# Linear attention and a multiplicative FFN on one core: the gate products of the last four chunks by Strassen's seven block products

## The chip, the core and the metric

The kernel runs on one core of a Trainium2 chip. The metric is the device time of one execution in microseconds (us); lower is better. The engines are TensorE (PE, which does all matrix products and writes their sums to PSUM), VectorE (DVE), ScalarE (ACT), GpSimd (POOL) and SyncE (SP, which here issues nearly all DMAs). Each engine works through its own instructions strictly in order, and waits for the others by semaphores. PSUM has eight banks of 128 partitions x 512 f32.

## The reference

```python
phi = lambda x: np.where(x > 0, x, np.exp(x) - 1.0) + 1.0
q_p, k_p = phi(q), phi(k)                       # q, k, v: 8 batches, 8 heads, 576 rows, 64 columns
kv  = einsum('bhsd,bhse->bhde', k_p, v)
num = einsum('bhsd,bhde->bhse', q_p, kv)
den = einsum('bhsd,bhd->bhs', q_p, k_p.sum(axis=2))[..., None] + 1e-06
x   = (num / den) as 4608 tokens x 512
a, b = x @ w1, x @ w2                           # the gates: 512 -> 1024
out = ((a * b) @ w3) @ w_out                    # 4608 x 512, f32
```

## The kernel before

The 4608 tokens are 9 chunks of 512 tokens (`c0` = 0 to 8), each of 4 tiles of 128 tokens (`t` = 0 to 35, `t = 4*c0 + m`). The product of w3 and w_out is formed once (wf), so that an output tile is `(a*b) @ wf`.

All work is written out by hand as a list of steps in the string ORDER (L21 to L61). Each step is a small function; the list is run from left to right, and what it issues stands on every engine's queue in that order. A name such as `F.3.4` is the kind (`s_F`) and its arguments; a last letter is the engine that does the copy (a: ACT, v: DVE, p: POOL, s: SP).

- Loads `LQ`, `LK`, `LV` (L164 to L179): 576 KB each, of q, k, v for one batch and one half of the heads, issued on SP into one of 13 buffers of the kind "ld". A buffer comes free (`give`) when its readers have run.
- `EX` (exp on ACT), `PT` and `PM` (two DVE passes) form phi; `VC` converts v to bf16.
- `KB` is the kv product on PE. `QD` transposes phi(q) of one batch half by a DMA transpose on SP (L386) into one of 4 buffers "qt".
- `NT` (L422) is num and den of three token tiles on PE: 48 small products into both of two double PSUM tiles (kind "at", two banks each), then three short DVE instructions to 1/den. `NM.t.0`, `.1`, `.2` (L437) are the divisions on DVE into "xn", and release the two tiles. `ND` is the same for one token tile.
- `XD.c0.m` transposes two token tiles of a chunk by a DMA transpose on SP (L463) into "xt".
- `F.c0.f` (L497) is one block of 128 of the 1024 gate columns for one chunk: 4 matmuls of 128x512 for a into a bank of the kind "mm" (four banks), 4 for b into another, an ACT copy of a to SBUF (L492), and a DVE product of that copy with b's bank (L494) into the chunk's tile "ab".
- `O.t` (L540) is one output tile: 8 matmuls of 128x512 from "ab" and wf, and a copy of the bank to SBUF by ACT or DVE (L543). `S.t` stores it by two DMAs of 128 KB (L549). `Q.35` is the last tile, in pieces.

PSUM is the four "mm" banks and the two double "at" tiles for the whole run. The first part of the list loads and prepares the weights, and treats batches 0 and 1 and chunk 0. The list of before from the step `PT.k.2.0` on:

```python
LV.3.1 O.3.a PT.k.2.0 LQ.2.0 S.0.s LQ.3.0 PM.k.2.0 PM.q.2.1 VC.2.0.v LV.4.1 F.1.0 F.1.1 PT.k.3.1
PM.q.3.1 VC.3.0.a F.1.2 VC.2.1.a PT.q.2.0 F.1.3 LK.3.0 EX.q.2.0 PM.q.2.0 LQ.5.1 S.1.s S.2.s ND.8
KB.2.a QD.2.0 EX.k.3.1 F.1.4 PT.q.3.0 EX.q.3.0 PT.k.3.0 PM.k.3.1 F.1.5 VC.3.1.v QD.2.1 EX.k.3.0
PM.k.3.0 QD.3.1 F.1.6 F.1.7 O.4.a PM.q.3.0 PT.q.5.1 QD.3.0 NT.9 KB.3.a O.5.a NM.9.0 O.6.a NM.9.1
NM.9.2 NT.12 NM.12.0 NM.12.1 NM.12.2 O.7.a XD.2.0 XD.2.1 LV.4.0 F.2.0 LQ.4.0 EX.q.5.1 F.2.1 NT.15
S.3.s F.2.2 NM.15.0 F.2.3 LK.4.1 F.2.4 PM.q.5.1 F.2.5 VC.4.0.a LQ.4.1 LK.4.0 PT.k.4.0 EX.k.4.0
PM.k.4.0 XD.3.0 PT.k.4.1 F.2.6 F.2.7 XD.3.1 LK.5.1 LK.5.0 F.3.0 PT.q.4.0 PT.q.4.1 F.3.1 EX.q.4.0
F.3.2 PT.k.5.1 LK.7.0 O.8.a PT.k.5.0 EX.k.4.1 NM.15.1 NM.15.2 F.3.3 S.4.s EX.q.4.1 PM.k.4.1 EX.k.5.0
LV.5.1 LV.6.0 S.5.s VC.4.1.v PM.q.4.0 EX.k.5.1 LQ.5.0 LV.5.0 S.6.s PM.k.5.1 F.3.4 PT.q.5.0 PM.q.4.1
S.7.s S.8.s VC.5.0.v O.9.a EX.q.5.0 O.10.a O.11.a LQ.7.1 VC.5.1.v PM.q.5.0 QD.4.0 F.3.5 F.3.6
PM.k.5.0 EX.k.7.0 KB.4.v PT.k.7.0 QD.4.1 S.9.s S.10.s S.11.s F.3.7 KB.5.a NT.18 XD.4.0 O.12.a
PM.k.7.0 NM.18.0 NM.18.1 XD.4.1 QD.5.1 NM.18.2 O.13.a O.14.v O.15.a F.4.0 F.4.1 F.4.2 F.4.3 VC.6.0.a
...
```

Attention (the steps `NT`, `NM`, `QD`) goes on beside the gates of chunks 1 to 7; `NM.33.2`, its last step, stands just before `F.7.0`.

## Time and profile before

| quantity | before |
| --- | --- |
| median of 3 runs | 240.42 us (240.42 to 240.85) |
| span of the profiled execution, first to last instruction | 239.7 us |
| PE busy | 233.2 us (97%) |
| DVE busy | 151.0 us (63%) |
| ACT busy | 115.0 us (48%) |
| POOL busy | 8.1 us (3%) |
| DMA, mean rate | 233 GB/s |

The time of the profiled execution itself is not given apart from its span; the median stands 0.7 us above the span. How to read the profile: the page splits the span into 40 slices of 6 us and gives each engine's busy share in tenths. The groups of instructions give for each line its busy time, the mean duration of one instruction, and the idle time ahead of it with what ended it. The chain of waits follows the end of the run back through whatever released each piece of work. The table by windows gives busy microseconds of each engine in a stretch, then the granted TensorE clock, the share of the 16 DMA engines that was busy (packets in flight side by side can take it above 1) and GB/s.

### The profile page before, as it was taken

What the parts mean: (1) busy time and instruction counts of PE and PEld (TensorE: products, weight loads), DVE (VectorE), ACT (ScalarE), POOL (GpSimd) and SP (SyncE); (2) the same over time, 40 slices, a digit from 0 to 9 for tenths busy, and PEclk for the clock granted to TensorE, in tenths of its full rate; (3) what the DMA queues carried; (4) which work ended last, traced back from release to release, by engine and by line L of the source; (5) the groups of instructions that cost most, each with busy time, mean ns of one, the idle gap of its engine ahead of it and who ended that gap; (6) DMA issues with size and microseconds to landing.
All of it is one profiled execution on the core that took longest, in us unless ns stands there. A gap on an engine that the chain in (4) does not pass through costs nothing.

```text
span 239.7 us, 5540 instructions
## 1 busy us (share of the span) xinstructions
PE 233.2 (97%) x2276; PEld 120.2 (50%) x2276; DVE 151.0 (63%) x278; ACT 115.0 (48%) x173; POOL 8.1 (3%) x15
## 2 busy tenths in 40 slices
PE   8899999999999999999999999999999999999994
...
DVE  0347787889999646877862588885546363433341
...
PEclk9999999999999999999999999999999999999999
DMA  6999999999996999999879959965293763005216
GB/s 241 402 406 397 379 375 390 390 390 389 396 332 137 158 357 247 323 406 296 190 106 192 392 123 262 320 116 131 52 178 69 174 157 88 3 0 125 50 24 154
DMA packets 52553, 55.81 MB, mean 233 GB/s; under 512 B 31280, under 2 KB 32560, under 8 KB 52528
## 3 DMA queue, kind: packets, MB, share of 16 engines
...
q10 hardware_dynamic: 240, 0.26, 0.3%
q14 instruction: 7, 0.06, 0.1%
...
## 4 chain that ended last, share of the span: by engine, by line
PE 96%; DVE 1%; ACT 1%; issue 0%
PE o_ps L536 26%; PE a_ps L483 25%; PE b_ps L483 24%; PE wf_ps L264 6%; PE nd L399 3%; PE w3p L252 3%; PE warm L149 2%; PE kbp L341 2%; PE a_ps L516 2%; PE b_ps L516 2%; PE xp L458 1%; PE qp L369 1%; PE kvp L341 1%; ACT wo_sb L218 0%; ACT w3b L238 0%; DVE w3t L253 0%
## 5 line engine op out<-in xcount | busy, mean ns | idle before, releaser
L483 PEld LDWEIGHTS <-w_sb 128*128 128x128 bf16 x544 | 52.6, 98 | 62.5 <-DVE xt L459 0.3
L494 DVE TENSOR_TENSOR ab<-a_sb,b_ps 128x512 bf16<-128x512 f32 x68 | 46.2, 686 | 39.9 <-PE b_ps L483 38.6
L492 ACT COPY a_sb<-a_ps 128x512 f32<-128x512 f32 x68 | 39.8, 586 | 64.0 <-PE a_ps L483 63.6
L483 PE MATMUL a_ps<-xt,w_sb 128*128 128x512 bf16 x272 | 69.9, 380 | 0.0
L483 PE MATMUL b_ps<-xt,w_sb 128*128 128x512 bf16 x272 | 69.8, 379 | 0.0
L536 PE MATMUL o_ps<-wf_sb,ab 128*128 128x512 bf16 (+2 forms) x304 | 65.2, 368 | 0.0
L536 PEld LDWEIGHTS <-ab 128*128 128x128 bf16 x304 | 28.4, 98 | 31.7 <-issue 0.4
L543 ACT COPY o_sb<-o_ps 128x512 f32<-128x512 f32 x22 | 12.9, 586 | 33.5 <-PE o_ps L536 26.7
L405 DVE TENSOR_TENSOR xn<-nd,r 128x512 bf16<-128x512 f32 (+2 forms) x47 | 23.8, 559 | 0.3
L274 ACT ACTIVATE ek<-k 128x1152 bf16<-128x1152 f32 x16 | 18.7, 1172 | 0.7 <-ACT ek L274 0.7
L274 ACT ACTIVATE eq<-q 128x1152 bf16<-128x1152 f32 x16 | 18.7, 1168 | 0.4 <-DMA q<-in_q_dram 0.4
L543 DVE COPY o_sb<-o_ps 128x512 f32<-128x512 f32 x13 | 9.0, 691 | 15.3 <-PE o_ps L536 12.6
L264 PE MATMUL wf_ps<-wo_sb,w3t 128*128 128x512 bf16 x64 | 15.6, 380 | 0.5 <-ACT wo_sb L218 0.5
L286 DVE TENSOR_SCALAR phq<-q 128x1152 bf16<-128x1152 f32 x16 | 12.0, 755 | 2.7 <-DMA q<-in_q_dram 2.7
L294 DVE TENSOR_TENSOR phk<-phk,ek 128x1152 bf16<-128x1152 bf16 x16 | 11.9, 750 | 1.8 <-ACT ek L274 1.7
L294 DVE TENSOR_TENSOR phq<-phq,eq 128x1152 bf16<-128x1152 bf16 x16 | 12.1, 755 | 1.0 <-ACT eq L274 0.8
L286 DVE TENSOR_SCALAR phk<-k 128x1152 bf16<-128x1152 f32 x16 | 12.0, 753 | 0.0
L264 PEld LDWEIGHTS <-w3t 128*128 128x128 bf16 x64 | 5.9, 98 | 5.8 <-issue 0.7
L328 ACT CAST vt<-v 128x1152 bf16<-128x1152 f32 x7 | 8.1, 1162 | 0.9 <-DMA v<-in_v_dram 0.9
L253 ACT CAST w3t<-w3p 128x512 bf16<-128x512 f32 x7 | 4.0, 587 | 9.3 <-PE w3p L252 7.4
L399 PEld LDWEIGHTS <-qt 64*64 64x64 bf16 x576 | 6.1, 106 | 4.3 <-issue 4.1
L399 PE MATMUL nd<-kv,qt 64*64 64x65 bf16 x576 | 7.6, 194 | 0.4 <-DVE w3t L253 0.4
...
## 6 DMA issues: line engine op xcount, KB each, us to landing
...
v<-in_v_dram SPq DMA_DIRECT2D x16, 576.0 KB, 10.5
...
```

The costliest lines, as they stand in the source:

```text
L264: nc.tensor.matmul(wfs[i], w3ts[i][:, c, :], wo_sb[:, c, :], start=(c == 0), stop=(c == FC - 1))
L274: nc.scalar.activation(out=t, in_=raw[n, b, h], func=AF.Exp)
L286: (nc.gpsimd if e == "p" else nc.vector).tensor_scalar(out=by_set(n, t), in0=by_set("k", raw[n, b, h]), scalar1=0.0, scalar2=1.0, op0=ALU. ...
L294: nc.vector.tensor_tensor(out=t, in0=t, in1=by_set("k", es[n, b, h]), op=ALU.min)
L399: nc.tensor.matmul(dst[g * R:(g + 1) * R], qts[b, a // 2][rows, j, a % 2 * R:(a % 2 + 1) * R], kvs[b][rows, a // 2, a % 2, :], start=True, ...
L405: nc.vector.tensor_tensor(out=xn[:, :, a0:a1], in0=n4[:, :, :, 0:D], in1=r.unsqueeze(3).to_broadcast([P, 2, a1 - a0, D]), op=ALU.mult)
L483: nc.tensor.matmul(ops_[key][:, tiles.start * P:tiles.stop * P], w[:, w_row(kc), f * P:(f + 1) * P], xts[c0][:, tiles, kc, :], start=(kc = ...
L492: nc.scalar.copy(out=a_sbs[c0, f], in_=ops_[key])
L494: nc.vector.tensor_mul(out=abs_[c0][:, f, :], in0=a_sbs[c0, f], in1=ops_[key])
L516: nc.tensor.matmul(p, w[:, w_row(kc), f * P:(f + 1) * P], xts[c0][:, 2 * g:2 * g + 2, kc, :], start=(kc == 0), stop=(kc == KC - 1))
L536: nc.tensor.matmul(o_ps, abs_[c0][:, f, m * P:(m + 1) * P], wf_sb[:, f, cols], start=(f == 0), stop=(f == FC - 1))
L543: copy_of(e)(out=o_sbs[t], in_=o_ps)
```

## The change

The gates of chunks 5 to 8 are formed in two pairs of chunks, (5, 6) and (7, 8). For a pair, each gate is a product of w (512 rows x 1024 columns, as two by two blocks of 256 x 512) with x of the two chunks (two by two blocks of 256 rows x 512 tokens). It is formed by seven block products in place of eight, in Winograd's form of Strassen's scheme, which needs four sums of blocks of w (`WS`, for w1 and w2) and four of blocks of x (`WT`, for each pair).

- A step `WP.c0.f.side.i` is block product i for block column f (0 to 3) and gate `side` (0: a, 1: b): two matmuls of 128x512. Products 1, 6, 7, 4 add up in one bank, 5 and 3 in a second, 2 stands in an "mm" bank. ACT copies the partial sums after products 1, 5, 6 (and, for gate a, after 4) to SBUF in f32. DVE adds such a copy to a bank after 2, 3, 7; for gate b each sum is then multiplied with gate a's in a second DVE instruction, and after 4 with the bank itself. The copies use the buffers of "e", "phk", "phq" and "a_sb".
- `WS` and `WT` are DVE additions and subtractions of 128 x 1024 bf16 in SBUF. The sums of w1 lie in wo_sb, whose first use is over; the other sums and the a*b blocks ("abq") take buffers of the kind "ld", and `O` reads a*b from there.
- `RB` closes the pool of the double tiles "at" and opens four single banks "bk" in their place, for the products. It stands after `NM.33.2`, so that all `NT` and `NM` are ahead of all `WP`.
- The list is new from `PT.k.2.0` on: `F.1` to `F.4`, attention of batches 2 to 7 and its loads and transposes stand ahead of `RB`; the `WP` steps, 20 `O` steps and `Q.35` behind it.

```diff
--- before.py
+++ after.py
+PAIRS = (5, 7)
+WIDE = ()
...
+XP.7.v LV.2.1 EX.k.2.0 PM.k.2.1 LV.3.1 O.3.a PT.k.2.0 PM.q.2.1 LQ.3.0 VC.3.1.v LK.3.0 PM.q.3.1 VC.3.0.a
+VC.2.0.v F.1.5 S.0.s F.1.7 LQ.2.0 EX.q.3.0 PM.k.2.0 LK.5.0 LV.5.1 LK.4.0 LQ.4.0 F.1.1 EX.k.3.0 PT.k.3.1
+PT.q.2.0 S.2.s EX.q.2.0 F.1.2 PT.k.3.0 PM.q.2.0 F.1.4 QD.2.1 VC.2.1.a F.1.6 PT.q.3.0 QD.2.0 ND.8
+PM.k.3.0 LQ.5.1 EX.k.3.1 KB.2.a F.1.0 LQ.4.1 PM.q.3.0 QD.3.1 PM.k.3.1 F.1.3 NT.9 NM.9.0 QD.3.0 NM.9.1
+LQ.5.0 KB.3.a PT.q.4.1 EX.q.5.1 O.7.a NM.9.2 EX.q.4.0 VC.5.1.v XD.2.0 S.1.s O.6.a PT.k.4.0 PT.q.5.1
+NT.12 EX.k.5.0 PT.k.5.0 XD.2.1 O.5.a NM.12.0 LV.4.1 PM.q.5.1 O.4.a PT.q.5.0 NM.12.1 NM.12.2 LK.4.1
+PT.q.4.0 EX.q.4.1 F.2.7 NT.15 LK.5.1 NM.15.0 LK.6.1 LK.6.0 LV.4.0 EX.k.4.1 WS.1.1.v F.2.5 XD.3.1
+VC.4.1.v PM.q.4.0 S.7.s PM.k.5.0 F.2.6 F.2.2 PM.q.4.1 F.2.4 WS.0.1.v LV.5.0 F.2.3 EX.k.4.0 WS.1.3.v
+PT.k.4.1 VC.4.0.a PM.k.4.0 XD.3.0 PT.k.5.1 F.2.1 LV.6.0 S.4.s S.5.s EX.q.5.0 PM.q.5.0 S.3.s LQ.7.0 F.3.4
+PM.k.4.1 F.2.0 NM.15.1 LQ.7.1 F.3.7 NM.15.2 EX.k.5.1 VC.5.0.v KB.4.v PM.k.5.1 WS.1.2.v QD.4.0 QD.4.1
+LV.7.1 EX.k.6.0 O.8.a PT.q.7.1 EX.k.6.1 PT.k.6.0 F.3.2 NT.18 WS.0.3.v LQ.6.1 QD.5.1 NM.18.0 LQ.6.0 S.8.s
+XD.4.0 KB.5.a VC.6.0.a F.3.5 PT.k.6.1 PM.k.6.0 F.3.3 EX.q.7.1 LK.7.0 PT.q.6.1 O.9.a NM.18.1 QD.5.0
+PT.q.7.0 NM.18.2 PM.k.6.1 S.6.s VC.7.1.v EX.q.7.0 PT.k.7.0 LK.7.1 F.3.6 XD.4.1 PT.q.6.0 O.10.a O.11.a
+EX.q.6.1 LV.6.1 NT.21 NM.21.0 F.4.1 NM.21.1 VC.6.1.v LV.7.0 F.3.1 PM.q.7.1 NM.21.2 F.3.0 XD.5.1 KB.6.v
+NT.24 EX.q.6.0 PM.q.6.0 PM.q.7.0 EX.k.7.1 QD.7.1 PM.q.6.1 S.11.s XD.5.0 F.4.2 WS.1.4.v NM.24.0 QD.6.0
+F.4.3 QD.6.1 WS.0.2.v EX.k.7.0 PM.k.7.0 S.10.s F.4.7 S.9.s PT.k.7.1 F.4.0 PM.k.7.1 NM.24.1 XD.6.0
+VC.7.0.a F.4.4 QD.7.0 NM.24.2 F.4.5 F.4.6 NT.27 NM.27.0 KB.7.a NM.27.1 NM.27.2 O.19.a NT.30 XD.6.1
+NM.30.0 NM.30.1 O.13.a NM.30.2 WT.5.1.v WT.5.2.v O.15.a WS.0.4.v NT.33 NM.33.0 WT.5.3.v NM.33.1 NM.33.2
+RB WP.5.0.0.1 WT.5.4.v WP.5.0.1.1 WP.5.0.0.5 WP.5.0.0.2 WP.5.0.0.6 WP.5.0.1.6 XD.7.0 WP.5.0.1.5
+WP.5.0.0.7 WP.5.0.0.3 WP.5.0.1.7 WP.5.0.1.3 O.14.v WP.5.1.0.1 WP.5.0.0.4 WP.5.1.0.5 WP.5.0.1.4
+WP.5.1.0.6 WP.5.1.1.1 WP.5.1.0.3 WP.5.1.1.5 WP.5.1.0.7 S.19.s WP.5.1.1.6 WP.5.0.1.2 WP.5.1.0.2
+WP.5.1.0.4 WP.5.1.1.7 XD.8.1 S.15.s WP.5.2.0.1 WP.5.2.0.2 S.14.s WP.5.1.1.3 WP.5.2.0.5 WP.5.1.1.4
+WP.5.2.0.6 XD.8.0 WP.5.1.1.2 WP.5.2.0.3 O.17.v WP.5.2.1.1 WP.5.2.0.7 XD.7.1 WP.5.3.0.1 WP.5.2.1.5
+WP.5.2.1.2 WP.5.2.1.6 WP.5.2.0.4 WP.5.3.0.6 WP.5.2.1.7 WP.5.2.1.3 S.13.s WP.5.3.0.2 WP.5.3.1.1 WT.7.3.v
+O.16.a WT.7.1.v WP.5.2.1.4 WP.5.3.0.5 WP.5.3.0.7 WP.5.3.1.2 WP.5.3.0.3 WT.7.2.v WP.5.3.1.6 WP.5.3.1.5
+O.12.a O.18.a WP.5.3.0.4 WP.5.3.1.7 S.17.s WP.5.3.1.3 WP.7.0.0.1 WP.7.0.0.5 WP.5.3.1.4 WP.7.0.0.6
...
+WP.7.2.1.7 WP.7.3.1.6 S.23.s O.24.a WP.7.3.1.5 WP.7.3.1.7 S.24.s WP.7.3.0.4 WP.7.3.1.2 WP.7.2.1.4
+WP.7.3.1.4 O.27.v O.30.a O.28.v S.27.s WP.7.3.1.3 O.31.v S.31.s S.30.s O.29.v O.33.v O.32.v S.28.s
+S.29.s S.33.s S.32.s O.34.a S.34.b Q.35
...
+    at_pool = ctx.enter_context(ExitStack())
+    pools = {"mm": ps, "at": at_pool.enter_context(tc.tile_pool(name="at", bufs=1, space=bass.MemoryType.PSUM))}
...
-    free = {"ld": deque(range(13)), "mm": deque(range(4)), "at": deque(range(2))}
+    at_pool = ctx.enter_context(ExitStack())
+    pools = {"mm": ps, "at": at_pool.enter_context(tc.tile_pool(name="at", bufs=1, space=bass.MemoryType.PSUM))}
+
+
+
+    free = {"ld": deque(range(13)), "mm": deque(range(4)), "at": deque(range(2)), "bk": deque(range(4))}
...
-        pool = ps if kind in ("mm", "at") else sb
+        pool = pools.get(kind, sb)
...
+    def ab_of(c0, f):
+        for c in range(2):
+            if c0 - c in PAIRS and c0 - c not in WIDE:
+                return quads[c0 - c, f % 4][:, c, f // 4]
+        return abs_[c0][:, f]
...
-            nc.tensor.matmul(o_ps, abs_[c0][:, f, m * P:(m + 1) * P], wf_sb[:, f, cols],
+            nc.tensor.matmul(o_ps, ab_of(c0, f)[:, m * P:(m + 1) * P], wf_sb[:, f, cols],
...
+        c0 = t // CT - (t // CT - 1 in PAIRS)
+        if c0 in PAIRS and c0 not in WIDE:
+            n = uses["o", c0] = uses.get(("o", c0), 0) + 1
+            if n == 2 * CT:
+                for f in range(FC // 2):
+                    give("ld", ("abq", c0, f))
...
+    quads, wsum, xsum, wbank, wtmp, uses = {}, {}, {}, {}, {}, {}
+
+    def late(key, n):
+        t = take("ld", key, [P, HW], F32, key[0]).bitcast(BF16)[:, 0:n * NCH]
+        return t
+
+    def w_half(w, k, fh):
+        return w[:, 2 * k:2 * k + 2, fh * NCH:(fh + 1) * NCH]
+
+    def x_half(c0, k):
+        return xts[c0][:, :, k::2, :]
+
+    def ws_of(side, i):
+        if side == 0:
+            return wo_sb.rearrange("p c n -> p (c n)").rearrange("p (i r n) -> p i r n", i=4, r=2)[:, i - 1]
+        key = ("ws", side, (i - 1) // 2)
+        if key not in wsum:
+            wsum[key] = late(key, 4).rearrange("p (i r n) -> p i r n", i=2, r=2)
+        return wsum[key][:, (i - 1) % 2]
+
+    def xs_of(c0, i):
+        key = ("xs", c0, (i - 1) // 2)
+        if key not in xsum:
+            xsum[key] = late(key, 4).rearrange("p (i m r n) -> p i m r n", i=2, m=CT, r=2)
+        return xsum[key][:, (i - 1) % 2]
+
+    def s_WS(side, i, e):
+        w = (w1_sb, w2_sb)[side]
+        a, b, op = {1: (w_half(w, 0, 1), w_half(w, 1, 1), ALU.add),
+                    2: (ws_of(side, 1), w_half(w, 0, 0), ALU.subtract),
+                    3: (w_half(w, 0, 0), w_half(w, 0, 1), ALU.subtract),
+                    4: (w_half(w, 1, 0), ws_of(side, 2), ALU.subtract)}[i]
+        (nc.gpsimd if e == "p" else nc.vector).tensor_tensor(out=ws_of(side, i), in0=a, in1=b, op=op)
+
+    def s_WT(c0, i, e):
+        b11, b12, b21, b22 = x_half(c0, 0), x_half(c0 + 1, 0), x_half(c0, 1), x_half(c0 + 1, 1)
+        a, b = {1: (b12, b11), 2: (b22, xs_of(c0, 1)), 3: (b22, b12), 4: (b21, xs_of(c0, 2))}[i]
+        (nc.gpsimd if e == "p" else nc.vector).tensor_tensor(out=xs_of(c0, i), in0=a, in1=b, op=ALU.subtract)
+
+    def w_mm(ps, c0, f, side, i, first):
+        w = (w1_sb, w2_sb)[side]
+        lhs = {1: lambda: w_half(w, 0, 0), 2: lambda: w_half(w, 1, 0), 3: lambda: ws_of(side, 4),
+               4: lambda: w_half(w, 1, 1), 5: lambda: ws_of(side, 1), 6: lambda: ws_of(side, 2),
+               7: lambda: ws_of(side, 3)}[i]()
+        rhs = {1: lambda: x_half(c0, 0), 2: lambda: x_half(c0, 1), 3: lambda: x_half(c0 + 1, 1),
+               4: lambda: xs_of(c0, 4), 5: lambda: xs_of(c0, 1), 6: lambda: xs_of(c0, 2),
+               7: lambda: xs_of(c0, 3)}[i]()
+        for r in range(2):
+            nc.tensor.matmul(ps, lhs[:, r, f * P:(f + 1) * P], rhs[:, :, r, :],
+                             start=(first and r == 0), stop=(r == 1), skip_group_check=not first)
+
+    def w_tmp(kind, name):
+        if kind == "a_sb":
+            return take(kind, None, [P, NCH], F32, name)
+        t = take(kind, None, [P, HW], BF16, name)
+        return t.bitcast(F32)[:, 0:NCH]
+
+    def w_ab(c0, f, c, g):
+        if c0 in WIDE:
+            if c0 + c not in abs_:
+                abs_[c0 + c] = take("ab", None, [P, FC, NCH], BF16, "ab")
+            return abs_[c0 + c][:, f + 4 * g]
+        if (c0, f) not in quads:
+            quads[c0, f] = late(("abq", c0, f), 4).rearrange("p (c g n) -> p c g n", c=2, g=2)
+        return quads[c0, f][:, c, g]
+
+    def w_add(c0, f, side, ps, tmp, c, g, e):
+
+        nc.vector.tensor_tensor(out=tmp, in0=ps, in1=tmp, op=ALU.add)
+        if side == 0:
+            wtmp[c0, f, "a", c, g] = tmp
+        else:
+            (nc.gpsimd if e == "p" else nc.vector).tensor_mul(
+                out=w_ab(c0, f, c, g), in0=wtmp.pop((c0, f, "a", c, g)), in1=tmp)
+
+    def s_RB(e):
+
+        at_pool.close()
+        pools["bk"] = at_pool.enter_context(tc.tile_pool(name="bk", bufs=1, space=bass.MemoryType.PSUM))
+
+    def s_WP(c0, f, side, i, e):
+        q = c0, f, side
+        bank = q + ("z" if i in (3, 5) else "x" if i == 2 else "y",)
+        if i == 2:
+            wbank[bank] = mm_tile("wx" + "ab"[side], bank)
+        elif i in (1, 5):
+            wbank[bank] = take("bk", bank, [P, NCH], F32, "w" + bank[3] + "ab"[side])
+        ps = wbank[bank]
+        w_mm(ps, c0, f, side, i, i in (1, 2, 5))
+        if i in (1, 5, 6):
+            t = wtmp[q + (i,)] = w_tmp({1: "e", 5: "phq", 6: "phk"}[i], "p" + str(i) + "ab"[side])
+            nc.scalar.copy(out=t, in_=ps)
+        elif i == 2:
+            w_add(c0, f, side, ps, wtmp.pop(q + (1,)), 0, 0, e)
+            give("mm", bank)
+        elif i == 3:
+            w_add(c0, f, side, ps, wtmp.pop(q + (6,)), 1, 0, e)
+            give("bk", bank)
+        elif i == 7:
+            w_add(c0, f, side, ps, wtmp.pop(q + (5,)), 1, 1, e)
+        elif side == 0:
+            t = wtmp[c0, f, "a", 0, 1] = w_tmp("a_sb", "p4a")
+            nc.scalar.copy(out=t, in_=ps)
+        else:
+            nc.vector.tensor_mul(out=w_ab(c0, f, 0, 1), in0=wtmp.pop((c0, f, "a", 0, 1)), in1=ps)
+        if i == 4:
+            give("bk", bank)
+        if i > 3:
+            n = uses[c0, i in (4, 7)] = uses.get((c0, i in (4, 7)), 0) + 1
+            if n == 4 * FC // 2:
+                give("ld", ("xs", c0, int(i in (4, 7))))
+        if side and i in (3, 5, 6, 7):
+            n = uses["s", side, i in (3, 7)] = uses.get(("s", side, i in (3, 7)), 0) + 1
+            if n == FC * len(PAIRS):
+                give("ld", ("ws", side, int(i in (3, 7))))
```

58 lines of the change are left out of this document (20 added, 38 removed).

## The prediction

> **What bounds the kernel now.** I read the page's table of slices first.
>
> ```profile
> PE   8899999999999999999999999999999999999994
> DVE  0347787889999646877862588885546363433341
> PEclk9999999999999999999999999999999999999999
> DMA  6999999999996999999879959965293763005216
> ```
>
> PE is full from the third slice to the last, at full clock. DMA is full for the first 25 slices (150 us) and half empty later; DVE has room in most slices. The chain of waits, and the groups of instructions:
>
> ```profile
> 59.93 0.86 PE a_ps L483 x4
> ...
> 76.95 0.76 PE kbp L341 x71
> ...
> 127.87 0.86 PE a_ps L483 x4
> ...
> 181.35 0.51 PE nd L399 x48
> 181.85 0.97 PE a_ps L483 x4
> ...
> 229.20 6.96 PE o_ps L536 x48
> ```
> ```profile
> L494 DVE TENSOR_TENSOR ab<-a_sb,b_ps 128x512 bf16<-128x512 f32 x68 | 46.2, 686 | 39.9 <-PE b_ps L483 38.6
> L492 ACT COPY a_sb<-a_ps 128x512 f32<-128x512 f32 x68 | 39.8, 586 | 64.0 <-PE a_ps L483 63.6
> L294 DVE TENSOR_TENSOR phk<-phk,ek 128x1152 bf16<-128x1152 bf16 x16 | 11.9, 750 | 1.8 <-ACT ek L274 1.7
> ```
>
> From 60 us on the chain is PE alone, without a gap: four matmuls of 128x512 take 0.864 us, 0.216 each. DVE and ACT wait for PE (38.6 and 63.6 us), not PE for them. So the time is PE's work, and PE's last matmul ends at 236.2 (229.20 + 6.96).
>
> **What the change takes from PE.** Four chunks of gates are 4 x 8 x 8 = 256 matmuls; 2 pairs x 4 columns x 2 gates x 7 products x 2 = 224 replace them. 32 x 0.216 = 6.9 us go. With PE still gapless the span would be 239.7 - 6.9 = 232.8, and with the 0.7 us by which the median stands above the span, **233.5**. The rest of this part asks whether PE stays gapless.
>
> **DVE's new load.** How DVE's instructions follow one another is read from its timeline:
>
> ```profile
> 60.26 0.76 DVE L286 TENSOR_SCALAR phk<-k 128x1152 bf16<-128x1152 f32 x1
> ...
> 73.64 0.75 DVE L294 TENSOR_TENSOR phk<-phk,ek 128x1152 bf16<-128x1152 bf16 x1
> 74.31 1.28 DVE L494 TENSOR_TENSOR ab<-a_sb,b_ps 128x512 bf16<-128x512 f32 x2
> 75.51 0.76 DVE L294 TENSOR_TENSOR phq<-phq,eq 128x1152 bf16<-128x1152 bf16 x1
> 76.17 0.76 DVE L286 TENSOR_SCALAR phq<-q 128x1152 bf16<-128x1152 f32 x1
> 76.85 0.17 DVE L431 TENSOR_SCALAR r<-nd 128x14 f32<-128x14 f32 x1
> 77.04 0.17 DVE L432 TENSOR_SCALAR r<-nd 128x10 f32<-128x10 f32 x1
> 77.25 0.30 DVE L433 RECIPROCAL r<-r 128x24 f32<-128x24 f32 x1
> 77.58 1.95 DVE L405 TENSOR_TENSOR xn<-nd,r 128x512 bf16<-128x512 f32 x4
> ```
>
> Starts lie 0.60 us apart for a 512-wide f32 product (1.20 for two), 0.67 for a 1152-wide pass, 0.73 for the three small ones of `NT` together, 1.86 for the `NM` of three tiles. A block sum (`WS`, `WT`: 1024 bf16 from two SBUF tiles) has no row; the nearest is L294, 1152 wide at 0.67, so 0.60; an f32 rate (0.60 per 512) would make it 1.1, and 16 of them 8 us more. The SBUF-only f32 products of gate b I price as L494 (0.69). Since each reads what the DVE instruction before it wrote, I let it wait for that one's end: 1.31 for the pair.
>
> Per block column DVE has 3 x 0.60 for gate a, 3 x 1.31 + 0.60 for gate b: 6.3 us. PE has 28 x 0.216 = 6.05. Alone that would make DVE the bound, but behind `RB` PE also has 20 `O` and `Q`: 48.4 + 20 x 1.73 + 2.4 = 85.3 us, against 62.6 of DVE (50.6 products, 3.0 `WT`, 8.9 copies). ACT has 56 copies of 0.59. So behind `RB` PE leads; I add nothing, and at most 2 us for the first pair, where few `O` lie between.
>
> Ahead of `RB` it is tight. From the last common step (PE free at 59.9 by the chain, DVE 0.67 after the start at 60.26, at 60.9) I count to `NM.33.2`: PE 32 `F` x 1.73 + 11 `O` x 1.73 + 9 `NT` x 0.61 + 6 `KB` x 0.78 (0.76 and its end) + 0.2 = 84.7 us, to 144.7. DVE: 43 passes `PT`/`PM` 28.8, 32 `F` 19.2, 27 `NM` 16.7, 9 `NT` 6.6, 7 `VC` 4.7, 8 `WS` and 3 `WT` 6.6, the rest 2.1: 84.7 as well, to 145.6. DVE has no room left.
>
> **The wait at `RB`.** The new banks lie where `NT.33`'s tiles are, so the first product waits for `NM.33`. From the end of `NT.30`, PE has O.13, O.15 and `NT.33` queued: 4.1 us. DVE has 0.73 + 1.86 for NT.30, WT.5.1, WT.5.2 and WS.0.4 (1.8), then NT.33's 0.73 and 2.46 with WT.5.3 inside: 7.6. Nothing covers the difference: PE stands 3.5 us, or 2.7 if the first half of the tiles suffices. I take 3.0.
>
> **The DMA queue** is where I expect the most. Every load, transpose and store goes through SP's one queue, and the new list pulls it forward.
>
> ```profile
> 68.51 9.08 SPq L386 DMA_TRANSPOSE qt<-phq  x4
> 78.30 3.21 SPq L463 DMA_TRANSPOSE xt<-xn  x2
> ...
> 115.20 3.85 SPq L549 DMA_DIRECT2D out_dram<-o_sb  x6
> 119.11 5.43 SPq L463 DMA_TRANSPOSE xt<-xn  x2
> 124.64 2.76 SPq L386 DMA_TRANSPOSE qt<-phq  x2
> ...
> 192.57 1.24 SPq L463 DMA_TRANSPOSE xt<-xn  x1
> ```
> ```profile
> 70.00:72.00 2.00, 2.00 (x11) 0.91 (x10) 2.00 (x4) 2.00 (x3) 0.00 (x0) 1.00 1.23 211
> 75.00:76.00 1.00, 1.00 (x6) 0.47 (x5) 1.00 (x2) 0.00 (x0) 0.00 (x0) 1.00 0.00 0
> 92.00:93.00 1.00, 1.00 (x6) 0.48 (x5) 0.04 (x1) 0.58 (x1) 0.00 (x0) 1.00 2.81 155
> 93.00:94.00 1.00, 1.00 (x7) 0.41 (x6) 1.00 (x2) 0.24 (x1) 0.00 (x0) 1.00 0.07 23
> 94.00:95.00 1.00, 1.00 (x6) 0.48 (x5) 0.63 (x2) 1.00 (x2) 0.00 (x0) 1.00 1.17 262
> 104.00:106.00 2.00, 2.00 (x11) 0.90 (x10) 2.00 (x6) 1.02 (x2) 0.00 (x0) 1.00 1.06 407
> 120.00:122.00 2.00, 2.00 (x90) 1.21 (x75) 1.60 (x6) 0.44 (x2) 0.00 (x0) 1.00 1.14 105
> ```
>
> A load is 0.59 MB; at the 400 GB/s of a full queue (row 104:106) that is 1.47 us, 1.43 at best. A store tile (0.26 MB) takes 0.7 among loads, 1.28 alone (six halves in 3.85). Two transposes took 3.21 us with nothing else queued, 2.76 in another pair; the pair behind loads at 92 us took about 3.5, for the engines moved next to nothing for over a microsecond as it began (23 GB/s at 93:94). I take 1.7 each, with ends of 1.25 (the shortest row) and 2.3 (9.08 / 4, waits for DVE within).
>
> The test of these prices is the list of before. From about 60.3 us (its 5 loads and 3 tiles, 9.5 us, reach to the 70 us at which the rate falls to 211 GB/s, with transposes) to XD.4.1, it has 18 loads, 12 tiles and 12 transposes: 26.5 + 8.4 + 20.4 = 55.3, to 115.6. The trace has those transposes moving at 120 to 122, with an empty queue at 75 to 76 and stores alone at 115. So the prices are rather low than high. They were in time, since `F.4.0` starts at 127.9 in the chain above.
>
> In the new list F.4.1, chunk 4's first, stands earlier: 22 `F`, 8 `O`, 5 `NT`, 4 `KB` and `ND.8` lie ahead of it, 38.0 + 13.8 + 3.1 + 3.1 + 0.2 = 58.2, so PE is there at 118.1. XD.4.1 must have landed by then, and ahead of it the queue holds 25 loads, 13 other transposes and 9 tiles: 36.8 + 14 x 1.7 + 6.3 = 66.9, to 127.2; with 1 us to land, 128.2. **PE is about 10.3 us late there**, in part already at F.2.7 and F.3.4, which wait for their own transposes in the same way (by the same count 4 and 6.5 us late). Whatever is behind in PE's order moves with it, and nothing in the list gives the time back. Later deadlines are milder: QD.6.1 for `NT.27` lands near 142 against 136.9, XD.6.1 for WT.5.1 near 149 against 142. All ends together: cheapest prices give 59.2 us and 2.4 late, dearest 81 us and 24 late.
>
> **Sum:** 233.5 + 10.5 (queue) + 3.0 (`RB`) = **247.0 us**, slower by 2.7%.
>
> **Rivals.** (1) *The queue keeps up*, on the other side of before. For it speaks that two transposes moved 240 to 290 GB/s once running (row 94:95). It decides when 14 transposes cost at most (118.1 - 60.3 - 36.8 - 6.3) / 14 = 1.05 us each, below every row; near the cheap ends it is 233.5 + 2.4 + 2.7 = 238.6, and with no lateness 236.5. [...] Chance 0.25, with a twentieth in it for the wait at `RB` being hidden too (below 236).
>
> (2) *Half the lateness*, prices between: 5 to 6 us late, 241 +- 1.5. Chance 0.10, of which 0.04 within 0.2% of before (what a measurement of this kernel tells from no change) and 0.06 slower.
>
> (3) *Worse than the forecast*: transposes at 2.3 us, loads held back because DVE, itself late, frees their buffers late, or PE's clock lowered by its own pauses. Each gives 253 or more: 14 x 0.6 = 8.4 us for the first. The trace of before has no pause of PE and no lower clock in its middle, so it cannot price the last. [...] Chance 0.10.
>
> (4) *The saving isn't there*, because a product that adds onto a bank waits for the copy before it. Of one gate and column the bank's chain is four products, two ACT copies and one DVE sum, 4 x 0.43 + 2 x 0.59 + 0.69 = 3.6 us; two gates interleave, while PE needs 6.05 for both, so it is covered. It would cost under 2 us, inside the forecast.
>
> **Chances and range.** Forecast (242 to 253) 0.55, rival 1 0.25, rival 2 0.10, rival 3 0.10. Faster 0.25; same 0.04; slower 0.55 + 0.06 + 0.10 = 0.71. The range, 236 to 253, leaves out the hidden case and rival 3, 0.15. The forecast's own range is 242 to 253.
>
> **What would show it.** Right: PE idle ahead of the `F` steps of chunks 2, 3 and most of all 4, ended by DMA xt<-xn; GB/s and DMA share full from 60 to about 145 us; `RB` near 155, with some 3 us of idle PE ahead of the first products, ended by DVE; a gapless PE behind. Matmuls at 0.216 and 32 fewer. Wrong: chunk 4's gates starting near 118, which would mean transposes near 1 us; or DVE rows of `WS`, `WT` near 1.1, or idle PE between products, which would move the loss behind or to DVE.

## The result, and the profile after

| quantity | before | after |
| --- | --- | --- |
| median of 4 runs | 240.57 us (240.42 to 240.85) | 256.92 us (255.51 to 258.97) |
| ratio to before, 95% interval | | 1.067 (1.061 to 1.0735) |
| span of the profiled execution | 239.7 us | 253.7 us |
| PE busy | 233.2 us | 231.0 us |
| DVE busy | 151.0 us | 190.0 us |
| ACT busy | 115.0 us | 127.5 us |
| mean granted TensorE clock, profiled execution | 0.999 | 0.984 |

The change makes the kernel 16.4 us slower. The sign, the place and two of the causes (the queue and the wait at `RB`) were forecast; the forecast size, 6.6 us, was too small, and the measured time lies 3.9 us above the range. The third cause, the clock, stood in the prediction only as a rival. The page's slices of after:

```profile
PE   8899999999797699897959998499999999999993
DVE  0556788988897869976599987768996866969631
PEclk9999999999999799999999999889999999999998
DMA  7999999999999999999994897115211203415166
```

PE has holes from the 11th slice (63 us) to the 26th (165 us), and none behind it. DMA is full for the first 21 slices, with no emptier slice between. In two places (the 14th slice, and the 26th and 27th) the granted clock drops while PE still has work, which it never did before.

The table by windows from 60 us on, of before and then of after (length, busy time of PE, PEld, DVE, ACT and POOL, clock, DMA share, GB/s):

```profile
60.00:260.00 200.00, 176.14 (x1664) 83.55 (x1662) 111.13 (x202) 76.25 (x117) 0.00 (x0) 0.99 0.65 166
```
```profile
60.00:260.00 200.00, 173.96 (x1630) 81.55 (x1628) 148.75 (x265) 88.19 (x141) 0.00 (x0) 0.97 0.66 166
```

Before, PE was idle for 239.7 - 60 - 176.1 = 3.6 us, its tail behind the last matmul. After, it is idle for 253.7 - 60 - 174.0 = 19.7 us. Its busy time fell by only 2.2 us, where 32 matmuls should have taken 6.9 away; 4.7 us came back inside the busy time. PE's timeline shows the pauses (start, duration, what; in brackets the idle time ahead of it and what ended that). These are the seven over 0.9 us that a transpose or the swap of the banks ended:

```profile
77.75 0.58 PE L414 MATMUL nd<-kv,qt 64*64 64x65 bf16 x48 [1.50 <-DMA qt<-phq]
...
84.98 0.56 PE L414 MATMUL nd<-kv,qt 64*64 64x65 bf16 x31 [1.94 <-DMA qt<-phq]
...
104.45 1.04 PE L498 MATMUL a_ps<-xt,w_sb 128*128 128x512 bf16 x4 [1.15 <-DMA xt<-xn]
...
115.32 0.26 PE L414 MATMUL nd<-kv,qt 64*64 64x65 bf16 x8 [1.25 <-DMA qt<-phq]
...
131.42 1.04 PE L498 MATMUL a_ps<-xt,w_sb 128*128 128x512 bf16 x4 [2.44 <-DMA xt<-xn]
...
154.51 0.45 PE L414 MATMUL nd<-kv,qt 64*64 64x65 bf16 x31 [0.92 <-DMA qt<-phq]
...
162.59 0.60 PE L642 MATMUL wya<-xt,w_sb 128*128 128x512 bf16 x2 [3.56 <-DVE xn L420]
```

They make 12.8 us; four more (1.38, 0.25 and 0.21 ended by DVE, 0.70 by a transpose) bring all pauses to 15.3. Transposes end 9.9 of that, the wait at `RB` is 3.56, other waits for DVE 1.8.

The rest of the lost time stands in the clock. The windows around its two drops:

```profile
83.00:84.00 1.00, 0.04 (x5) 0.00 (x0) 1.00 (x3) 1.00 (x2) 0.00 (x0) 1.00 0.24 45
84.00:85.00 1.00, 0.02 (x4) 0.02 (x4) 0.65 (x1) 0.45 (x1) 0.00 (x0) 1.00 1.13 358
85.00:86.00 1.00, 1.00 (x33) 0.66 (x34) 0.55 (x3) 0.00 (x0) 0.00 (x0) 0.57 1.08 356
86.00:88.00 2.00, 2.00 (x6) 0.64 (x5) 2.00 (x5) 0.00 (x0) 0.00 (x0) 0.50 1.20 325
88.00:89.00 1.00, 1.00 (x5) 0.47 (x4) 1.00 (x2) 0.09 (x1) 0.00 (x0) 0.72 1.01 161
...
161.00:163.00 2.00, 0.41 (x2) 0.21 (x3) 2.00 (x5) 0.00 (x0) 0.00 (x0) 1.00 0.00 0
163.00:164.00 1.00, 1.00 (x5) 0.45 (x4) 0.13 (x1) 0.77 (x2) 0.00 (x0) 0.82 0.21 48
164.00:167.00 3.00, 3.00 (x8) 1.06 (x7) 0.69 (x1) 1.54 (x4) 0.00 (x0) 0.50 0.70 159
167.00:168.00 1.00, 1.00 (x6) 0.43 (x5) 0.00 (x1) 1.00 (x2) 0.00 (x0) 0.97 0.00 0
```

Shortly after the pause of 1.94 us and after that of 3.56 us the granted clock is halved for some 3.4 us; such a stretch is called a spell below. Each spell loses 1.7 us (0.43 + 1.00 + 0.28, and 0.18 + 1.50 + 0.03), 3.4 together. That is most of the 4.7 us of busy time; 1.3 us stay untraced. As an account, then, the span grew by -6.9 (matmuls) + 15.3 (pauses) + 3.4 (clock) + 1.3 (untraced) + 0.8 (a tail of 4.3 us behind the last matmul in place of 3.5) = 13.9 of the 14.0 us seen. An account is not yet a cause: what the first spell costs, ahead of waits for transposes, is a question to the experiments.

### The profile page after: what moved, and what is told of

It is laid out like the page before. It is cut to its first block, busy times and chain, and to the rows that moved or that the text cites. A ratio compares the mean times of both kernels' runs of the same rounds, so it can differ in the third digit from the quotient of the medians.

```text
span 253.7 us, 5564 instructions
## 1 busy us (share of the span) xinstructions
PE 231.0 (91%) x2244; PEld 118.2 (47%) x2244; DVE 190.0 (75%) x342; ACT 127.5 (50%) x197; POOL 7.6 (3%) x15
## 4 chain that ended last, share of the span: by engine, by line
PE 57%; DVE 17%; DMA 15%; SPq 4%; issue 3%; ACT 2%; DVEq 0%
PE o_ps L557 16%; DMA qt<-phq 9%; PE wf_ps L279 6%; PE wyb L642 5%; PE wya L642 5%; DMA xt<-xn 4%; DVE ab L509 4%; PE a_ps L498 4%; PE b_ps L498 3%; PE wzb L642 3%; DVE xn L420 3%; PE wza L642 2%; PE w3p L267 2%; PE warm L164 2%; DMA v<-in_v_dram 2%
## 5 line engine op out<-in xcount | busy, mean ns | idle before, releaser
L498 PEld LDWEIGHTS <-w_sb 128*128 128x128 bf16 x288 | 27.6, 98 | 38.0 <-DMA xt<-xn 4.2
L498 PE MATMUL a_ps<-xt,w_sb 128*128 128x512 bf16 x144 | 37.0, 379 | 3.6 <-DMA xt<-xn 3.6
L557 PE MATMUL o_ps<-wf_sb,ab 128*128 128x512 bf16 x160 | 38.5, 391 | 0.0
L498 PE MATMUL b_ps<-xt,w_sb 128*128 128x512 bf16 x144 | 36.9, 379 | 1.4 <-DVE ab L509 1.4
L564 ACT COPY o_sb<-o_ps 128x512 f32<-128x512 f32 x22 | 12.8, 588 | 38.8 <-PE o_ps L557 31.6
L507 ACT COPY a_sb<-a_ps 128x512 f32<-128x512 f32 x36 | 21.0, 586 | 19.9 <-PE a_ps L498 18.4
L557 PE MATMUL o_ps<-wf_sb,abq 128*128 128x512 bf16 (+2 forms) x144 | 29.1, 355 | 0.0
L509 DVE TENSOR_TENSOR ab<-a_sb,b_ps 128x512 bf16<-128x512 f32 x36 | 24.3, 682 | 6.2 <-ACT a_sb L507 3.1
L557 PEld LDWEIGHTS <-ab 128*128 128x128 bf16 x160 | 15.4, 100 | 18.1 <-issue 1.9
L557 PEld LDWEIGHTS <-abq 128*128 128x128 bf16 x144 | 13.5, 98 | 14.5
L564 DVE COPY o_sb<-o_ps 128x512 f32<-128x512 f32 x13 | 8.9, 688 | 10.9 <-PE o_ps L557 10.8
L642 PEld LDWEIGHTS <-w_sb 128*128 128x128 bf16 x96 | 9.4, 99 | 14.9 <-DVE xn L420 3.7
L414 PE MATMUL nd<-kv,qt 64*64 64x65 bf16 x576 | 8.3, 196 | 6.9 <-DMA qt<-phq 6.3
## 6 DMA issues: line engine op xcount, KB each, us to landing
wb<-in_moe_w_dram SPq DMA_DIRECT2D x4, 512.0 KB, 10.8
```

Source lines behind the costliest of these rows:

```text
L414: nc.tensor.matmul(dst[g * R:(g + 1) * R], qts[b, a // 2][rows, j, a % 2 * R:(a % 2 + 1) * R], kvs[b][rows, a // 2, a % 2, :], start=True, ...
L498: nc.tensor.matmul(ops_[key][:, tiles.start * P:tiles.stop * P], w[:, w_row(kc), f * P:(f + 1) * P], xts[c0][:, tiles, kc, :], start=(kc = ...
L507: nc.scalar.copy(out=a_sbs[c0, f], in_=ops_[key])
L509: nc.vector.tensor_mul(out=abs_[c0][:, f, :], in0=a_sbs[c0, f], in1=ops_[key])
L557: nc.tensor.matmul(o_ps, ab_of(c0, f)[:, m * P:(m + 1) * P], wf_sb[:, f, cols], start=(f == 0), stop=(f == FC - 1))
L564: copy_of(e)(out=o_sbs[t], in_=o_ps)
```

## The experiments

Each diff is against the kernel that the text builds on: the changed kernel where nothing else is said. The changed kernel was not measured again beside the experiments. The kernel before was, and its medians lie between 240.57 and 241.41 us, so that times of different groups compare to about 1 us.

Three questions: is it the queue or DVE that makes PE late ahead of `RB`, what do the swap of the banks and the clock cost, and does the scheme itself pay where its needs don't crowd the queue?

### The queue: loads, stores, and the order without the scheme

**e1_halfload** leaves 12 of the loads out: for q, k and v of batches 4 to 7, the half of the heads that stands second in the list reads the buffer of the other half. So it also takes fewer of the 13 buffers; **e2_nostore**, next, changes the queue alone.

```diff
+        if key[0] in ("q", "k", "v") and key[1] >= 4:
+            base = key[0], key[1], "both"
+            if base in raw:
+                raw[key] = raw[base]
+                return
```

> The changed kernel, but the second load of each pair (q, k or v of one batch from 4 on) is left out and its steps read the first one's data: 12 loads of 576 KB fewer, 10 of them ahead of XD.4.1. All PE, DVE and ACT work stays. Queue theory (the DMA queue is behind by what it has to carry ahead of chunk 4): 10 x 1.47 = 14.7 us less to carry, so the PE pauses ended by DMA (9.9 us in the changed kernel) go almost entirely, the first product after the bank swap starts near 148 to 151 in place of 162.6, and the time is 243 to 247. DVE theory (84.7 us of DVE in 84.7 us of PE is the real bound): the first product is not earlier than about 158 and the time stays above 252.

Measured: 245.40 us (245.12 to 245.67), ratio 1.017 (1.014 to 1.021). PE's timeline at the first product, and the windows of the swap:

```profile
153.73 0.60 PE L657 MATMUL wya<-xt,w_sb 128*128 128x512 bf16 x2 [3.56 <-DVE xn L435]
```
```profile
150.00:154.00 4.00, 0.44 (x25) 0.21 (x11) 3.93 (x10) 0.28 (x1) 0.00 (x0) 1.00 0.00 0
154.00:157.00 3.00, 3.00 (x16) 1.34 (x15) 0.97 (x2) 2.46 (x5) 0.00 (x0) 1.00 0.81 127
```

The first product starts 8.9 us earlier (153.73 against 162.59). That is less than the 148 to 151 that was expected, though the time lies within the queue theory's range. No `F` step waits for its transpose any more; the pauses come to 8.6 us, among them the same 3.56 at `RB` and two of 1.5 for qt. The clock stays at 1.00 in the whole profiled run, behind the 3.56 us pause too. Of the 10.4 us of span won (253.7 to 243.3) 8.9 lie ahead of the first product, and 1.5 behind it, where the second spell of the clock is gone.

**e2_nostore** leaves the 24 stores of tiles 0 to 11 out (the steps `S.0.s` to `S.11.s`).

```diff
-PT.q.2.0 S.2.s EX.q.2.0 F.1.2 PT.k.3.0 PM.q.2.0 F.1.4 QD.2.1 VC.2.1.a F.1.6 PT.q.3.0 QD.2.0 ND.8
+PT.q.2.0 EX.q.2.0 F.1.2 PT.k.3.0 PM.q.2.0 F.1.4 QD.2.1 VC.2.1.a F.1.6 PT.q.3.0 QD.2.0 ND.8 PM.k.3.0
...
```

> The changed kernel without the 24 stores of output tiles 0 to 11 (they are left out), which stand ahead of XD.6.1 on SP's queue, 9 of the 12 tiles ahead of XD.4.1. Queue theory: 9 x 0.7 to 1.28 = 6 to 11 us less ahead of chunk 4, the first product 5 to 9 us earlier, time 248 to 252. DVE theory: the stores have no part in it, 256 to 258.

Measured: 250.48 us (249.87 to 251.09), ratio 1.038 (1.034 to 1.043): 6.4 us went with the stores, within the queue theory's range. The first product starts 5.7 us earlier. The wait at `RB` stays, and so does the spell at half clock behind it (158 to 161 us):

```profile
156.89 0.60 PE L641 MATMUL wya<-xt,w_sb 128*128 128x512 bf16 x2 [3.53 <-DVE xn L419]
```

**e5_reorder** keeps the new list up to `NM.33.2` but not the scheme: no `WS`, `WT`, `RB` and `WP`; plain `F` steps of chunks 5 to 8 stand behind `NM.33.2`.

```diff
-PAIRS = (5, 7)
+PAIRS = ()
...
-PT.q.4.0 EX.q.4.1 F.2.7 NT.15 LK.5.1 NM.15.0 LK.6.1 LK.6.0 LV.4.0 EX.k.4.1 WS.1.1.v F.2.5 XD.3.1
+PT.q.4.0 EX.q.4.1 F.2.7 NT.15 LK.5.1 NM.15.0 LK.6.1 LK.6.0 LV.4.0 EX.k.4.1 F.2.5 XD.3.1 VC.4.1.v
...
```

> The new list without the new arithmetic: loads, transposes, attention and chunks 1 to 4 stand as in the changed kernel up to NM.33.2 (without the 11 block sums, 6.6 us of DVE), then chunks 5 to 8 by plain F steps, eight blocks in place of seven, and no bank swap. Queue theory: chunk 4's first gate starts near 131 as in the changed kernel and NM.33.2 ends near 160; behind it 6.9 us more of PE work, but no pause at the swap (3.5) and no clock drop there (1.7): time 257 to 261. DVE theory: with 6.6 us less on DVE ahead of NM.33.2 the stretch shortens by about as much, 250 to 254.

Measured: 258.19 us (257.96 to 258.43), ratio 1.070 (1.066 to 1.0735). The order alone is as slow as the whole change, although DVE has lost the 11 block sums that stood ahead of `RB`. Chunk 4's gates start where they did in after (131.42), and for the same reason:

```profile
131.26 1.17 PE L486 MATMUL a_ps<-xt,w_sb 128*128 128x512 bf16 x4 [2.20 <-DMA xt<-xn]
```

`NM.33.2` ends at 163.7, where it ended at 162.5 in after; 160 was expected. So the theory that DVE's full load is the main cause falls: less DVE work made neither point earlier, fewer transfers gave 6 and 12 us.

### The swap of the banks, and the clock

**e3_fill** moves O.14 and O.17 between `NT.33` and `RB`, so that PE has work while DVE finishes the divisions; ACT copies them.

```diff
-NM.30.0 NM.30.1 O.13.a NM.30.2 WT.5.1.v WT.5.2.v O.15.a WS.0.4.v NT.33 NM.33.0 WT.5.3.v NM.33.1 NM.33.2
+NM.30.0 NM.30.1 O.13.a NM.30.2 WT.5.1.v WT.5.2.v O.15.a WS.0.4.v NT.33 O.14.a O.17.a NM.33.0 WT.5.3.v
...
```

> The changed kernel with the output tiles O.14 and O.17 moved from behind the bank swap to between NT.33 and NM.33 (copied by ACT in place of DVE): 3.5 us of PE work where PE stands 3.56 us for NM.33.2. Swap theory: the pause goes, and with it the clock drop behind it (four to eight matmuls pairs at half speed, 1.7 us): time 251 to 253.5. If the pause only moves behind the swap, because DVE is as late as before and the two tiles are missing there: 255.5 or more.

Measured: 254.37 us (253.68 to 256.53), ratio 1.056 (1.051 to 1.061). That is 2.6 us won, between the two expectations. The pause at `RB` and the clock's drop behind it are gone (the two spells of its profile lie at 85 and 116 us, ahead of waits for transposes), but the two tiles are missing later, among the products:

```profile
169.84 0.59 PE L642 MATMUL wza<-xs,wo_sb 128*128 128x512 bf16 x2 [0.90 <-DVE p6b L662]
...
179.84 0.59 PE L642 MATMUL wya<-xt,w_sb 128*128 128x512 bf16 x2 [0.30 <-DVE abq L698]
...
181.77 0.59 PE L642 MATMUL wzb<-xs,ws 128*128 128x512 bf16 x2 [1.34 <-DVE p6a L662]
```

Here the products wait for DVE's sums: 2.5 of the 3.56 us are given back.

**e10_halffill** does the same to e1_halfload (the diff is against that kernel).

```diff
-NM.30.0 NM.30.1 O.13.a NM.30.2 WT.5.1.v WT.5.2.v O.15.a WS.0.4.v NT.33 NM.33.0 WT.5.3.v NM.33.1 NM.33.2
+NM.30.0 NM.30.1 O.13.a NM.30.2 WT.5.1.v WT.5.2.v O.15.a WS.0.4.v NT.33 O.14.a O.17.a NM.33.0 WT.5.3.v
...
```

> e1 and e3 together: 12 loads left out (steps read the other half's data) and two output tiles moved into the wait at the bank swap. If queue and swap are two separate costs: e1's 245.4 less the 2.5 that e3 won, 242 to 244, that is, back near the kernel before, with the 6.9 us of the scheme eaten by what is left. If the rest is DVE alone (pauses ended by DVE or by transposes that wait for DVE), about 5 us of PE pauses remain ahead of the swap or behind it.

Measured: 244.95 us (244.90 to 245.01), ratio 1.015 (1.012 to 1.019), 0.45 us below e1_halfload, whose two runs lie 0.55 us apart. The 242 to 244 were missed. The same three pauses (0.90, 0.30, 1.34) come back behind the swap, one of 0.81 appears elsewhere, and e1_halfload's profiled run had no drop of the clock there that could be saved. So filling the swap by itself gave half a microsecond at most; the 2.1 us more in e3_fill are about the price of one spell of the clock, 1.7. The second reading of the expectation fits better: of the 7.5 us of pauses that are left 5.1 are ended by DVE, so once the queue is relieved, DVE is what PE waits for next.

**e4_warm** puts eight matmuls on zeros (16 records in the trace) between `NT.33` and `RB`, whose results nobody reads: PE stays late, but is not idle.

```diff
-NM.30.0 NM.30.1 O.13.a NM.30.2 WT.5.1.v WT.5.2.v O.15.a WS.0.4.v NT.33 NM.33.0 WT.5.3.v NM.33.1 NM.33.2
+NM.30.0 NM.30.1 O.13.a NM.30.2 WT.5.1.v WT.5.2.v O.15.a WS.0.4.v NT.33 H.8.0 NM.33.0 WT.5.3.v NM.33.1
...
```

> The changed kernel with 8 matmuls on zeros (128x256 f32, 0.46 us each, of no use) between NT.33 and the bank swap, on PE alone. The wait for NM.33.2 stays as long as it was. Clock theory: the granted clock no longer drops behind the swap, the products there run at 0.216 per matmul from the first one, and the time is 1.7 us less than the changed kernel's, 254 to 256. If the drop does not come from the pause: no change, 256 to 258.

Measured: 255.65 us (253.83 to 256.79), ratio 1.061 (1.058 to 1.065). Its timeline and its window behind the swap:

```profile
158.90 3.72 PE L164 MATMUL warm<-zero 128*128 128x256 f32 x16
162.54 0.61 PE L642 MATMUL wya<-xt,w_sb 128*128 128x512 bf16 x2
```
```profile
163.00:166.00 3.00, 3.00 (x15) 1.35 (x14) 0.77 (x2) 2.66 (x6) 0.00 (x0) 1.00 0.67 153
```

The first product starts at the same time as in after (162.54 and 162.59), and behind it the clock is 1.00 in place of 0.50; from there to the end it takes 89.5 us in place of 91.1, the price of one spell. So the drop follows from PE's idleness, and it costs time. The runs spread by 3 us, so the median alone would not have shown it; but all four runs of e4_warm have a mean clock of 0.982 to 0.989, and those of the changed kernel 0.971 to 0.984.

The same run shows the other case. Ahead of `RB` it has a spell that after's profile doesn't have, behind a pause of 2.59 us:

```profile
114.00:121.00 7.00, 4.41 (x130) 2.77 (x130) 3.62 (x8) 2.56 (x6) 0.00 (x0) 0.76 0.96 265
```

At a mean clock of 0.76 these 7 us lose 1.7, of which PE works through 1.4, and yet the first product isn't later. The next wait for a transpose, at F.4.1, is shorter for it (1.50 us in place of 2.44): where the queue sets the time, a slower PE only waits less. Of after's two spells the second is thus shown to cost 1.7 us, and the first, at 85 us, most likely cost nothing: e5_reorder's profile has no spell there, and its chunk 4 starts only 0.16 us earlier (131.26 and 131.42).

### The scheme for the last pair alone

**e6_pair78** takes before's list up to chunk 6 and forms only chunks 7 and 8 by the seven products, 16 matmuls less (3.46 us). Its transfers keep before's places, but for `XD.8`, which now stands ahead of `RB`.

```diff
-PAIRS = (5, 7)
+PAIRS = (7,)
...
+S.21.s O.24.a S.22.s O.25.a S.23.s RB WP.7.0.0.1 WP.7.0.0.2 WP.7.0.1.1 WP.7.0.1.2 WT.7.1.v WT.7.2.v
+WT.7.3.v WT.7.4.v WP.7.0.0.6 WP.7.0.0.5 WP.7.0.1.6 WP.7.0.1.5 WP.7.0.0.7 WP.7.0.0.3 WP.7.0.1.7
...
```

> The list of before up to NM.27, with Strassen for the one pair (7, 8) only: no load or transpose is pulled forward but XD.8, O.24 to O.27 and O.23 cover the bank swap and the wait for XD.8, and 56 products replace the 16 F steps of chunks 7 and 8. PE has 16 matmuls less, 3.5 us. Theory that the scheme itself is sound and only the list's pull on the queue and the swap cost time: 237 to 239.5, faster than before by 0.5 to 1.5%. Rival, that the products' chains (DVE 6.3 us per column against 6.05 of PE, with two tiles to fill) cost more than they save: 240.5 or more.

Measured: 254.22 us (253.60 to 255.62), ratio 1.0545 (1.0515 to 1.057): slower than before (241.33 beside it) by 12.9 us, where a gain was expected. From 60 us to the swap one pause of 0.74 us is all; the products themselves wait:

```profile
197.07 1.03 PE L636 MATMUL wya<-xs,wo_sb 128*128 128x512 bf16 x2 [3.03 <-DVE xs L625]
...
224.96 0.59 PE L636 MATMUL wyb<-xt,w_sb 128*128 128x512 bf16 x2 [2.54 <-DVE p6b L656]
```

The first waits for block sums that stand behind the swap, the second for the chain product, ACT copy, DVE sum. In 192 to 236 us the clock's mean is 0.88 and PE is busy for 33.2 of 44 us. So 10.8 us are idle, and two spells (6.8 and 3.4 us at half clock, of which PE works 9.3) lose 4.6. The block sums `WT` stood behind `RB` there, and only two `O` tiles among the 56 products.

**e7_pair78p** gives six of gate b's products to POOL (`.p`; the diff is against e6_pair78).

```diff
-WP.7.0.1.7 WP.7.0.1.3
+WP.7.0.1.7.p WP.7.0.1.3.p
...
```

> As e6, with 6 of gate b's products of two SBUF tiles (after block products 3 and 7 of the first three columns) on POOL in place of DVE, 6 x 0.6 to 0.7 us off DVE. If DVE holds PE back between the products: 0.5 to 2 us less than e6. If PE's own work is the bound there: within 0.5 us of e6, or slower where POOL's products come late for the output tiles.

Measured: 250.90 us (250.35 to 251.17), ratio 1.039 (1.037 to 1.042). It is 3.3 us better, more than the 2 us expected at most, and the waits for block sums (3.02 us) and for the chain are still there. Most of the gain is the clock: its profile has one spell, which loses 1.7 us in place of 4.6, while PE's idle time among the products fell by 1.5 (10.8 to 9.2).

**e8_pairB** uses the changed kernel's own order of products for its first pair, puts O.23 to O.27 among them, three of the four sums `WT` ahead of `RB`, and attention's last steps with their transposes earlier (the diff is against e6_pair78).

```diff
-S.21.s O.24.a S.22.s O.25.a S.23.s RB WP.7.0.0.1 WP.7.0.0.2 WP.7.0.1.1 WP.7.0.1.2 WT.7.1.v WT.7.2.v
+F.6.6 WS.1.4.v WT.7.3.v F.6.7 RB WP.7.0.0.1 WT.7.4.v WP.7.0.1.1 WP.7.0.0.5 WP.7.0.0.2 WP.7.0.0.6
...
```

> Strassen for the pair (7, 8) alone, with the products in the order that ran without pauses in the changed kernel for its first pair (two columns interleaved, five output tiles O.23 to O.27 between them), attention's last three steps moved ahead of F.6.2 so that XD.8 and the block sums are done before the swap, and no load pulled forward. If e6 lost its time to product chains without cover and to late XD.8 and block sums: PE gapless, 16 matmuls less (3.5 us), 236.5 to 238.5, faster than before by 0.8 to 1.6%. If the scheme's chains cannot be covered with five tiles: pauses of 1 to 3 us between the products remain, 239 or more.

Measured: 239.95 us (239.39 to 240.55), ratio 0.994 (0.992 to 0.996). Faster than before, though 1.5 us short of the first expectation; the time is that of the second (239 or more), but the pauses among the products are under 0.6 us each. Its whole list of pauses behind 60 us:

```profile
161.99 1.89 PE L551 MATMUL o_ps<-wf_sb,ab 128*128 128x512 bf16 x8 [0.78 <-ACT a_sb L501]
...
220.17 0.59 PE L636 MATMUL wyb<-xs,w_sb 128*128 128x512 bf16 x2 [0.42 <-DVE p5b L656]
...
222.83 12.52 PE L551 MATMUL o_ps<-wf_sb,abq 128*128 128x512 bf16 x73 [0.56 <-DVE abq L692]
```

From e6_pair78 to here it is the same arithmetic and the same transfers; the order, with the choice of engine for a few copies, is worth 14 us; e8_pairB's profile has no spell, so 4.6 of them are the clock.

**e9_pairBp** adds the six products on POOL (the diff is against e8_pairB).

```diff
-WP.7.0.1.6 WP.7.0.1.5 WP.7.0.0.7 WP.7.0.0.3 WP.7.0.1.7 WP.7.0.1.3 O.23.a WP.7.1.0.1 WP.7.0.0.4
+WP.7.0.1.6 WP.7.0.1.5 WP.7.0.0.7 WP.7.0.0.3 WP.7.0.1.7.p WP.7.0.1.3.p O.23.a WP.7.1.0.1 WP.7.0.0.4
...
```

> As e8 with 6 of gate b's products of two SBUF tiles on POOL in place of DVE. If DVE is what holds the products back in e8, up to 2 us less than e8; otherwise the same within 0.5 us.

Measured: 239.66 us (239.27 to 240.62), ratio 0.994 (0.992 to 0.996), with the same three pauses. DVE is not what limits this version. The groups show the product of two f32 tiles in SBUF on both engines:

```profile
L660 POOL TENSOR_TENSOR abq<-p5a,p5b 128x512 bf16<-128x512 f32 x3 | 3.8, 1274 | 165.3 <-DVE p5b L656 165.3
...
L660 DVE TENSOR_TENSOR abq<-p1a,p1b 128x512 bf16<-128x512 f32 x4 | 2.8, 696 | 0.1
```

**e11_pairC** and **e12_pairD** go after the three pauses; their diffs are against e9_pairBp. e11_pairC spreads the last exps further back and puts O.27 between the last products:

```diff
-NM.24.2 QD.6.0 EX.q.7.0 PM.q.7.0 EX.q.7.1 S.16.s S.17.s F.5.6 PM.q.7.1 F.5.7 O.18.a KB.7.a NT.27 QD.7.1
+NM.24.2 QD.6.0 S.16.s S.17.s F.5.6 EX.q.7.0 F.5.7 PM.q.7.0 O.18.a KB.7.a EX.q.7.1 NT.27
...
```

> e9 with its three last pauses (0.78 at an ACT copy behind two exps, 0.42 and 0.55 at the end of the products) given cover: the exps spread between the gates, O.27 put between the last products. If those pauses are what is left of the lost saving: 1 to 1.7 us less than e9, 238 to 239. If the pauses only move: 239 to 240.

Measured: 240.76 us (239.59 to 242.46, 12 runs), ratio 0.9985 (0.9955 to 1.0015), no difference from before, and above both expectations. The three pauses are gone, and one takes their place, since phi and with it `QD.7` are now late:

```profile
171.91 0.38 PE L408 MATMUL nd<-kv,qt 64*64 64x65 bf16 x23 [2.30 <-DMA qt<-phq]
```

e12_pairD leaves the first exp where it was, moves the second one only past F.5.6, lets DVE copy O.18, and keeps O.27's new place:

```diff
-NM.24.2 QD.6.0 EX.q.7.0 PM.q.7.0 EX.q.7.1 S.16.s S.17.s F.5.6 PM.q.7.1 F.5.7 O.18.a KB.7.a NT.27 QD.7.1
+NM.24.2 QD.6.0 EX.q.7.0 S.16.s S.17.s F.5.6 PM.q.7.0 EX.q.7.1 F.5.7 PM.q.7.1 O.18.v KB.7.a NT.27 QD.7.1
...
-WP.7.3.0.5 WP.7.3.0.7 WP.7.3.1.2 WP.7.3.0.3 WP.7.3.1.6 WP.7.3.1.5 S.25.s O.26.a S.26.s O.27.a WP.7.3.0.4
-WP.7.3.1.7 WP.7.3.1.3 WP.7.3.1.4 S.27.s O.28.a O.30.v O.29.a S.28.s O.31.v S.30.s O.32.a S.29.s O.33.v
+WP.7.3.0.5 WP.7.3.0.7 WP.7.3.1.2 WP.7.3.0.3 WP.7.3.1.6 WP.7.3.1.5 S.25.s O.26.a S.26.s WP.7.3.0.4
+WP.7.3.1.7 WP.7.3.1.3 O.27.a WP.7.3.1.4 S.27.s O.28.a O.30.v O.29.a S.28.s O.31.v S.30.s O.32.a S.29.s
```

> The list of e9_pairBp with three changes: one exp of the last quarters (EX.q.7.1) moves between F.5.6 and F.5.7 and the first one stays where it is, so that QD.7 isn't late; O.18 is copied by VectorE in place of ScalarE; O.27 stands between the last products. If the three pauses that e9 has left (0.78, 0.42 and 0.55 us, 1.75 together) are what separates it from its count of matmuls, the time falls by 1.0 to 1.7 us, to 238 to 239 (ratio to the kernel before near 0.989). If they only move, as in e11_pairC, it stays at 239 to 240.5 and the trace shows other pauses of 1.5 us or more in their place.

Measured: 238.48 us (238.12 to 239.11, 6 runs) against 241.16 for the kernel before beside it, ratio 0.990 (0.988 to 0.992). One pause is left, and the stretch of the products is gapless:

```profile
171.53 1.04 PE L492 MATMUL a_ps<-xt,w_sb 128*128 128x512 bf16 x4 [0.77 <-DMA xt<-xn]
```
```profile
186.00:226.00 40.00, 40.00 (x187) 18.16 (x186) 26.33 (x42) 18.65 (x34) 7.49 (x6) 1.00 0.20 47
```

The gain now has an account: 16 matmuls are 3.46 us, less the 0.77 us pause is 2.69; the medians differ by 2.68. That these agree to a hundredth is chance, since the runs of either kernel spread by about 1 us. This version beats both kernels.

## Why the prediction was half right

**What held.** The bound (PE), the saving of 32 x 0.216, the mechanism and most of the places. PE idle ahead of chunk 3's and chunk 4's `F` steps, ended by DMA xt<-xn; a full queue from 60 to 130 us; a wait at `RB` ended by DVE; a gapless PE behind it: each is in the rows above. The wait that was forecast ahead of chunk 2's `F` steps did not come; before them PE waited for qt (1.50 and 1.94 us). The block sums follow one another in the 0.60 us assumed (starts at 158.16, 158.77 and 159.37 in after). e1_halfload, e2_nostore and e5_reorder confirm the queue, and e5_reorder takes DVE's tally of 84.7 us out as a cause of its own.

**What failed** is the size, and two steps of the sum failed most. The queue's price up to chunk 4 was too low, most likely in the transposes, taken at 1.7 us each; chunk 4 started 3.2 us later than forecast. And the clock, which PE's own pauses lower, was put at nothing in the sum; it took 1.7 us behind `RB`, and probably as much again in the median. The forecast's own stretches against the measured ones (a first product at 144.7 + 10.3 + 3.0 = 158.0 was forecast, PE's last matmul ends at 249.4):

| stretch | forecast | measured | too low by |
| --- | --- | --- | --- |
| to F.4.1 | 128.2 | 131.4 | 3.2 |
| from there to the first product | 29.8 | 31.2 | 1.4 |
| from there to PE's last matmul | 85.3 | 86.8 | 1.5 |
| tail behind it | 3.5 | 4.3 | 0.8 |
| outside the span | 0.7 | 1.8 | 1.1 |
| median against the profiled run | 0 | 1.4 | 1.4 |

That is 9.4 us; the stretches add up to 247.5, where the sum, made by differences, gave 247.0. The prediction has two slips in it: 128.2 less 118.1 is 10.1, which it writes as 10.3 and adds as 10.5, and its cheapest prices make 59.6 (25 x 1.43 + 14 x 1.25 + 9 x 0.7), not 59.2.

*The queue's price* is the largest term. F.4.1 was forecast to be 10.3 us late against PE's 118.1, and was 13.3 late. The windows of after from 60 to 130 us:

```profile
60.00:100.00 40.00, 34.94 (x440) 16.54 (x439) 32.69 (x61) 22.60 (x34) 0.00 (x0) 0.96 1.12 310
100.00:130.00 30.00, 25.67 (x344) 12.06 (x342) 22.41 (x41) 18.10 (x25) 0.00 (x0) 1.00 1.11 296
```

and of before:

```profile
60.00:100.00 40.00, 40.00 (x474) 19.14 (x473) 30.81 (x58) 23.11 (x36) 0.00 (x0) 1.00 1.01 274
100.00:130.00 30.00, 30.00 (x322) 14.23 (x321) 20.98 (x38) 16.31 (x24) 0.00 (x0) 1.00 0.97 241
```

The engines carried 40 x 36 + 30 x 55 KB = 3.1 MB more than before by 130 us, some five loads, and it was still not enough. If the prices of loads and stores hold, the 3.2 us over 14 transposes put one near 1.9 us, where 1.7 was taken from between 1.25 and 2.3. The prediction had the sign of it: its test on before's list came out at 115.6, where the trace has those transposes at 120 to 122. It called its prices "rather low than high" and kept them; the same shortfall for each of the 14 transposes would have added 5 us or more. The rival by which the queue keeps up needed 1.05, and no run comes near it.

*From F.4.1 to the first product* the wait for qt at `NT.27` (0.92 us), which the sum passed over as milder, and the rest of the wait at `RB` came on top: 3.56 us, the upper of the two values worked out (3.5 or 2.7). The 3.0 was a mean of the two; that the first half of the tiles suffices did not hold.

*Behind the first product* the term is the clock: 1.7 us by after's windows, and by e4_warm. It was the third rival, right as a mechanism, with a chance of 0.10 and no place in the sum, because the trace of before has no pause and could not price it. But a forecast that puts PE idle in several places needs a term for what that does to the clock. What the profiled run gives for it is 1.7 us of lost PE time for each of its two spells, one behind a pause of 1.94 us and one behind 3.56 us; the pause of 2.44 us between them was followed by none.

*The median against the profiled run* is likely the clock as well. The four runs of after have spans of 253.7, 254.7, 255.6 and 257.2 us at mean clocks of 0.984, 0.976, 0.971 and 0.971; the profiled one is the shortest, at the highest clock. A difference of 0.013 is 3.3 us lost in 256, about two spells. There is no trace of the other three, so where their spells lie stays open.

*The outside of the span* was read from two numbers that did not belong together: the median of 240.42 less the span of a profiled run that was itself about 1.1 us above that median. In nearly all later runs the time is 1.7 to 2.1 us above its own span (255.51 and 253.7 for after, 241.03 and 239.3 for before; two runs have 2.5 and 3.0).

*The fourth rival*, the uncovered product chains, stayed under its 2 us in after, where 15 `O` tiles lie among the 112 products. That bound was no property of the scheme: with two tiles among 56 products and another order the chains made 7.7 us of e6_pair78's pauses (10.8 less the 3.03 for block sums), and with two tiles taken away it gave 2.5 us back in e3_fill. DVE's products from SBUF, priced as L494 at 0.69, took 0.69 to 0.70.

*Which pause is followed by a drop of the clock* can be read from the traces. In each of them the clock changes only at times that lie whole multiples of 3.41 us apart (in after at 85.14, 88.55, 163.64 and 167.06 us: 1, 22 and 1 steps), and where these steps begin differs from run to run. A drop goes with how little PE works in the step ahead of it. The steps around `RB`, of after and then of e1_halfload, where the same pause of 3.56 us is cut in two by the end of a step:

```profile
160.23:163.64 3.41, 1.05 (x5) 0.51 (x6) 2.90 (x6) 0.41 (x1) 0.00 (x0) 1.00 0.00 0
163.64:167.06 3.42, 3.42 (x9) 1.22 (x8) 0.69 (x1) 1.96 (x5) 0.00 (x0) 0.50 0.67 153
```
```profile
148.36:151.78 3.42, 1.81 (x55) 0.86 (x52) 3.32 (x9) 0.78 (x2) 0.00 (x0) 1.00 0.10 22
151.78:155.19 3.41, 1.46 (x7) 0.70 (x8) 2.49 (x6) 0.82 (x2) 0.00 (x0) 1.00 0.08 19
155.19:158.60 3.41, 3.41 (x17) 1.56 (x16) 1.84 (x3) 2.31 (x5) 0.00 (x0) 1.00 0.78 137
```

In all 14 traces, from 60 us to PE's last matmul, the nine steps at full clock with at most 1.42 us of PE work are each followed by a step at half clock. Of the four with 1.46 to 1.56 us two are, and of those with more none is. So in these traces a pause counted by where in the steps of 3.41 us it fell, which also fits the two groups of e11_pairC's runs, though only one of those has a trace.

**Not settled:** the 1.3 us of busy time in after that stay untraced, and where the spells of its other three runs lie. Not tried: a second queue for the stores, or a list for two pairs that keeps before's transfers in their places.
